# Products of zeros in TensorE's waits ahead of attention's first unit, in place of two memsets, and a fifth block of the second layer ahead of its first output product

## The chip, the cores and the metric

The kernel runs on one core of one Trainium2 chip. The metric is device time of one launch in microseconds (us). The core has TensorE (PE, with PEld for its weight loads), VectorE (DVE), ScalarE (ACT), GpSimd (POOL) and SyncE (SP), which issues most DMAs. Engines run their own instruction lists in order and wait for each other by semaphores.

## The reference, cut to what matters

Three stages follow each other: a gated recurrence (4 batches, 8 heads, 768 steps, 40 dimensions), a mixture of experts in which each of 8 experts takes exactly 384 of 3072 tokens, and a dense two-layer network.

```python
for t in range(S):                                  # attention
    m_new = np.maximum(f_gate[:, :, t] + m, i_gate[:, :, t])
    f_stab = np.exp(f_gate[:, :, t] + m - m_new)
    i_stab = np.exp(i_gate[:, :, t] - m_new)
    C = f_stab * C + i_stab * outer(v_t, k_t);  n = f_stab * n + i_stab * k_t
    y[:, :, t] = sigmoid(o_gate[:, :, t]) * (C @ q_t) / max(abs(n @ q_t), 1.0)
...
for idx in np.argsort(-(x @ w_gate).flatten()):     # routes: best free pair first
    ...
out[mask] = np.maximum(x[mask] @ w1[e], 0.0) @ w2[e]          # per expert e
...
h = x @ w_in                                        # 320 -> 2048
g = np.where(h > 0.0, h, np.exp(np.minimum(h, 0.0)) - 1.0)
return g @ w_out                                    # 2048 -> 320
```

## The kernel before, in words

**Attention** works in 24 units, each 64 steps of 16 of the 32 sequences. For a unit TensorE makes the scores (`scores`, 32 small float32 products into `pS`), the decay matrix (`decay`, into `pF`), the reads of the state (`recall`, into `pR`), the values (`values`, into `pO`) and the new state (`state`, into `pC`). ACT turns the decay matrix into `W` (L321), DVE multiplies scores and `W` into `P` (`weigh`, L360) and copies or adds the new state into `C` (`add_state`, L421 and L419), POOL makes the faded keys `kt`.

Ahead of the units, `__init__` prepares the gates. It starts with `spin(SPIN)`: twelve products of the zero tile `wz` into a scratch bank (L145), which nobody reads. Then the first two time blocks' gates go through DVE (`maximum`, `logs`) and, split into three bfloat16 parts, through ACT and DVE in turns (`split`, L259 to L264, and L267 for `fb`). TensorE's list there is `scores(0)`; `decay(0)` in three pieces, the mask (L315), eight products of `sel` and `fp` (L317) and the one of `fb` (L319); `decay(1)`, which has the same bank `pF` and so waits until ACT has read it (L321); `scores(1)`; then `decays(1, 2)` and the units. DVE's list from there is the gate scan of the remaining steps (L235), the two memsets of the banks `pC` and `pX` (L218, L219), `P` of unit 0, a small product (L328), `P` of unit 1, five wide gate operations (`logs(2, NS)`, L244 to L250), and then the copy of unit 0's state (L421). The first `recall` of TensorE waits for that copy.

**The experts and the dense layers** run in 8 rounds of 384 tokens (TK). `P1` and `C1` are the expert's two layers, `P2` the first dense layer in 16 blocks of 128 columns (eight products of 384 columns each, `up`, L1242), `C2` its second (nine products of 320 columns for a block, L1387, L1388 and L1395). A block of `P2` takes one of four PSUM banks (NPH, `ph`). From the bank, `elu` makes on ACT a relu and an exp into a tile `e` (L1291, L1292; three such tiles), on DVE the sum (L1295, which frees the bank), on ACT or DVE the rounded part `gh` (L1112 or L1114) and on DVE the rest `gl` (L1119, which frees `e`). `C2` takes `gh` for six products, then `gl` for three. There are five tiles each of `gh` and `gl`.

The order is written by a planner. `main` makes a list of blocks: `C2` of block g comes LAG (three) blocks behind `P2`. `Plan` carries a time `t` for TensorE and one for each other engine, from fixed costs per instruction; each `elu` step is put on its engine's list when that time says it is due, and between the products `run` lets other work onto the lists: the routing of later rounds (`routes`, whose products are L805 to L847 and whose DVE steps include `ge`, L630), the splitting of weights and the gathering of rows. In a round the second layer's list begins with `P2` of blocks 0, 1 and 2 interleaved, `P2` 3, `C2` 0, `P2` 4, `P2` 5, `C2` 1, `C2` 2.

Of the kernel before, what the change touches and what calls it, by code (L numbers as in the profile page):

```python
# [31 lines left out]
TG = 20  # L32
NB, NL, PX = 2, 3, 0.2
WARM = [8, 2, 2, 2]


class Plan:
# [50 lines left out]
    def next(self):  # L88
        self.due(min(self.todo)[0])
# [30 lines left out]
class Attention:  # L120
# [4 lines left out]
    def __init__(self, nc, tc, consts, qk, vk, ig, fg, wg, xd, L, ident):  # L125
# [5 lines left out]
        V, G, A = nc.vector, nc.gpsimd, nc.scalar  # L131
# [6 lines left out]
        junk = self.psum("pF", 1)  # L138
        wz = self.wz = one.tile([128, 512], BF, name="wz")
        V.memset(wz, 0.0)  # L140

        def spin(n):

            for _ in range(n):
                nc.tensor.matmul(junk, wz[:, :128], wz, start=True, stop=True)  # L145

        spin(SPIN)
        warm = one.tile([1, 8], F32, name="warm")
        V.memset(warm, 0.0)
# [63 lines left out]
        self.opens(0)  # L213
        self.both(self.scores(0))
        self.load_qk(4)
        self.decay(0)
        self.maximum(128, S)
        V.memset(self.pC, 0.0)  # L218
        V.memset(self.pX, 0.0)  # L219
        self.decay(1)  # L220
        self.both(self.scores(1))
        self.weigh(0)
# [84 lines left out]

        return one

    def decay(self, u):  # L310

        A, PE = self.nc.scalar, self.nc.tensor
        n, bp = divmod(u, 2)
        p = self.psum("pF", 1)
        PE.matmul(p, self.idb, self.low, start=True, stop=False)  # L315
        for h in range(8):
            PE.matmul(p[:, h], self.sel[:, bp * 8 + h].rearrange("p r t -> p (r t)"), self.fp[:, n * 64:n * 64 + 64],  # L317
                      start=False, stop=False)
        PE.matmul(p, self.fb[:, n].rearrange("p r t -> p (r t)"), self.one_m[:, bp * 8:bp * 8 + 8], start=False, stop=True)  # L319
        self.W[u] = self.two.tile([128, 8, 64], F32, name="W", bufs=3)  # L320
        A.activation(self.W[u], p, AF.Exp)  # L321

# [605 lines left out]
class Mlp:  # L928
# [245 lines left out]
    def spin(self, n):  # L1174

        for _ in range(n):
            self.nc.tensor.matmul(self.junk, self.wih[:, 0, :128], self.wih[:, 0, :512], start=True, stop=True)
# [6 lines left out]
    def prep_x(self, r):  # L1184
# [6 lines left out]
        def turn(k):  # L1191
            for t in range(3):
                if (r, t) == (0, 0):
                    self.twice(k, 0)
                nc.tensor.transpose(ps[k][0][:, t * 128:t * 128 + 128], self.xg[k][:, t * 128:t * 128 + 128], self.ident)  # L1195

        def split(k):
            p, slot = ps[k]
            p = p.rearrange("p (t n) -> p t n", t=3)
            h, l = (x[:, :, k * 128:k * 128 + 128] for x in (xh, xl))  # L1200

            def rest():
                nc.vector.tensor_tensor(l, p, h, op=ALU.subtract)
                slot[0] = plan.on("d", 552)
                if k == 2:
                    self.xst[r] = (xh, xl)
                    self.xready[r] = slot[0]

            if r:
                plan.later(self.copy(h, p, 480, 555), rest)  # L1210
            else:
                nc.scalar.activation(h, p, AF.Copy)
                plan.on("a", 480)
                rest()

        if r == 0:
            ps = [self.psum() for t in range(3)]
            for k in range(3):
                self.spin(WARM[k])
                turn(k)  # L1220
                split(k)
            self.spin(WARM[3])
            return
# [208 lines left out]
    def main(self):  # L1432
        plan = self.plan
        LAG = 3
        items = []
        for r in range(NR):
            a, b = [], []
            for f in range(0, 8 + LAG, 2):
                if f < 8:
                    a += [(self.P1, r, f), (self.P1, r, f + 1)]  # L1440
                a += [(self.C1, r, g) for g in (f - LAG, f + 1 - LAG) if 0 <= g < 8]
            for f in range(0, 16 + LAG, 2):
                if f == 0:
                    b.append((self.P2, r, [0, 1, 2]))
                elif f == 2:
                    b.append((self.P2, r, [3]))
                elif f < 16:
                    b += [(self.P2, r, [f]), (self.P2, r, [f + 1])]
                b += [(self.C2, r, g) for g in (f - LAG, f + 1 - LAG) if 0 <= g < 16]
            if r:  # L1450
                tail = items[-LAG:]
                del items[-LAG:]
                items += a[:2] + tail[:2] + a[2:3] + tail[2:] + a[3:]
            else:
                items += a
            items += b
        items[-NL:] = [(lambda r, f: self.C2(r, f, NL), NR - 1, 16 - NL)]
        while items:
            if items[0] == (self.P1, items[0][1], 0) and self.xready.get(items[0][1], 1e18) > plan.t:
                k = next((k for k, x in enumerate(items[:7]) if x[0] == self.C2), 0)  # L1460
                items.insert(0, items.pop(k))
            fn, r, f = items.pop(0)
            if fn in (self.P1, self.C1):
                while r not in self.xst:
                    if self.plan.todo:
                        self.plan.next()
                    plan.t += 50
                    yield "rows" if self.routed >= r else "routes"
                while self.wsplit < 5 * r + (3 if fn == self.P1 else 4 + f // 4):
                    plan.t += 50  # L1470
                    yield "weights"
                if fn == self.P1 and f == 0:
                    plan.wait(self.xready[r])
            if fn == self.C2 and r == 0:
                while self.wdone < f + 1:
                    plan.t += 50
                    yield "wout"
            if fn == self.C1 and f == C0:
                self.rush = True
            g = f[0] if fn == self.P2 else f  # L1480
            self.pos = r + (g / 32 if fn in (self.P1, self.C1) else 3 / 8 + g * 5 / 128)
            yield from fn(r, f)
            if fn == self.C2 and f == C9:
                self.rush, self.prog = False, r
# [227 lines left out]
```

## Time and profile before

| | us |
|---|---|
| median of 3 runs | 749.46 |
| lowest, highest | 748.71, 754.47 |
| profiled execution, its own time | 749.06 |
| its span, first to last instruction | 747.3 |

The span is 1.8 us shorter than that execution's own time; the times below count from the span's start. Attention lasts to about 150 us, the routing of the first round to about 184 us, and the eight rounds fill the rest. TensorE matmul is busy for 697.3 us in 7244 products, with as many weight loads, and the chain of work that ended last is 74% TensorE. In the views, "idle before <- X" is the time an engine had nothing to do before an instruction and what released it; "issue" is a wait for which the profile shows no releaser. The clock column of a stretch is TensorE's granted clock, 1.00 for 2.4 GHz and 0.50 for 1.2 GHz.

### The profile page before, as it was taken

The numbers are of one execution on the slowest core, as the hardware profiler recorded it, in microseconds if no ns is written. First come the engines' busy times: TensorE is split into PE (matmuls) and PEld (weight loads), VectorE is DVE, ScalarE is ACT, GpSimd is POOL, SyncE is SP. The second block draws the span as 40 slices with busy tenths as digits, with TensorE's granted clock in tenths as the row PEclk, the third lists the DMA queues.
The fourth block names the chain that finished last, engine by engine and source line by source line (L and its number), as shares of the span: only waits on it lengthen the run. The fifth ranks groups of instructions, "written<-read, shape, count | busy, mean of one in ns | idle before, by whom it ended". The sixth has DMA issues, their size and how long they took to land.

```text
span 747.3 us, 18041 instructions
## 1 busy us (share of the span) xinstructions
PE 697.3 (93%) x7244; PEld 642.1 (86%) x7244; DVE 552.6 (74%) x1654; ACT 394.3 (53%) x892; POOL 192.2 (26%) x242
## 2 busy tenths in 40 slices
PE   7788889846999999999999999999999999999997
PEld 4566566734989998999899999999999999999997
DVE  7677968876888978996897688768867863752542
ACT  5554544434454726662675367456736763752443
POOL 4655745326211400410121022104100441001001
PEclk9899999956999999999999999999999999999999
DMA  8777967335101400310230023003200531100000
GB/s 277 224 221 223 280 201 232 88 107 184 59 1 41 168 2 1 131 63 17 74 109 28 1 86 97 28 1 111 75 24 0 175 113 68 36 1 27 1 1 26
DMA packets 22435, 67.29 MB, mean 90 GB/s; under 512 B 3536, under 2 KB 7632, under 8 KB 22352
## 3 DMA queue, kind: packets, MB, share of 16 engines
q1 hardware_dynamic: 14240, 35.12, 15.3%
q0 software_dynamic: 8064, 30.94, 12.6%
q8 instruction: 56, 0.92, 0.5%
q14 instruction: 27, 0.22, 0.1%
q10 hardware_dynamic: 48, 0.10, 0.0%
HBM read 58.28 MB, written 7.86 MB: 89 GB/s over the span
## 4 chain that ended last, share of the span: by engine, by line
PE 74%; issue 10%; DVE 9%; ACT 2%; DMA 2%; POOL 1%; POOLq 0%; SPq 0%; DVEq 0%; ACTq 0%
PE ph L1242 30%; PE acc L1395 6%; PE acc L1387 6%; PE acc L1388 6%; PE acc L1343 2%; PE pO L381 2%; PE pR L395 2%; PE acc L1337 2%; PE acc L1338 2%; PE pX L464 2%; PE acc L1335 1%; PE acc L1344 1%; PE pS L306 1%; PE ph L1195 1%; DMA vk<-in_vk_dram 1%
## 5 line engine op out<-in xcount | busy, mean ns | idle before, releaser
L1295 DVE SCALAR_TENSOR_TENSOR e<-e,ph 128x384 f32<-128x384 f32 x128 | 70.2, 549 | 45.9 <-ACT e L1292 45.4
L1291 ACT ACTIVATE e<-ph 128x384 f32<-128x384 f32 x128 | 62.3, 487 | 76.5 <-PE ph L1242 67.3
L1242 PE MATMUL ph<-yh,wih 128*128 128x384 f32 x256 | 87.7, 343 | 0.0
L1242 PE MATMUL ph<-yh,wil 128*128 128x384 f32 x256 | 86.3, 337 | 0.0
L1119 DVE TENSOR_TENSOR gl<-e,gh 128x384 fp32r<-128x384 f32 x128 | 70.0, 551 | 2.3 <-ACT gh L1112 1.0
L1259 ACT ACTIVATE gh<-ph 128x384 fp32r<-128x384 f32 x62 | 30.4, 490 | 74.2 <-PE ph L1242 74.1
L1292 ACT ACTIVATE e<-e 128x384 f32<-128x384 f32 x128 | 67.3, 526 | 4.0
L1424 POOL DMA_INDIRECT out_dram<-ot,idx x24 | 24.7, 1030 | 160.0 <-ACT ot L1112 157.0
L1242 PE MATMUL ph<-yl,wih 128*128 128x384 f32 x256 | 65.2, 341 | 0.0
L1123 POOL DMA_INDIRECT stg<-in_w1a_dram,wi x16 | 15.9, 996 | 191.4 <-DVE wi L864 188.6
L1266 DVE SCALAR_TENSOR_TENSOR gl<-ph,gh 128x384 fp32r<-128x384 f32 x64 | 35.0, 552 | 38.4 <-ACT gh L1259 38.1
L1387 PE MATMUL acc<-woh,gh 128*128 128x320 f32 x186 | 56.2, 313 | 0.0
L1112 ACT ACTIVATE gh<-e 128x384 fp32r<-128x384 f32 x95 | 48.8, 514 | 13.4 <-DVE e L1295 13.2
L1388 PE MATMUL acc<-wol,gh 128*128 128x320 f32 x186 | 55.5, 309 | 0.0
L1387 PE MATMUL acc<-woa,gh 128*128 128x320 f32 x168 | 51.8, 318 | 0.5 <-DVE gh L1114 0.5
L1388 PE MATMUL acc<-wob,gh 128*128 128x320 f32 x168 | 50.4, 309 | 0.0
L1242 PEld LDWEIGHTS ph<-yh,wih 128*128 128x128 f32 x256 | 48.1, 188 | 0.2
L1242 PEld LDWEIGHTS ph<-yh,wil 128*128 128x128 f32 x256 | 48.2, 188 | 0.0
L1242 PEld LDWEIGHTS ph<-yl,wih 128*128 128x128 f32 x256 | 45.4, 188 | 0.0
L1242 PE MATMUL ph<-xh,w1h 128*128 128x384 f32 x128 | 43.6, 341 | 0.7 <-ACT xh L1112 0.7
L1242 PE MATMUL ph<-yh,wis 128*128 128x384 f32 x128 | 44.1, 344 | 0.0
L1242 PE MATMUL ph<-yl,wis 128*128 128x384 f32 x128 | 43.2, 337 | 0.0
(311 smaller groups left out, 2059.4 us busy)
## 6 DMA issues: line engine op xcount, KB each, us to landing
vk<-in_vk_dram SPq DMA_DIRECT2D x24, 484.0 KB, 5.4
qk<-in_qk_dram SPq DMA_DIRECT2D x20, 320.0 KB, 5.0
cx<-in_win_dram SPq DMA_DIRECT2D x8, 512.0 KB, 4.9
xd<-x SPq DMA_DIRECT2D x48, 80.0 KB, 3.6
wx<-in_wout_dram SPq DMA_DIRECT2D x9, 320.0 KB, 2.9
cx<-in_wout_dram SPq DMA_DIRECT2D x5, 448.0 KB, 3.9
qk<-in_qk_dram SPq DMA_DIRECT2D x4, 512.0 KB, 7.1
cx<-in_win_dram SPq DMA_DIRECT2D x4, 256.0 KB, 4.6
```

Of the source, the lines that this page charges most:

```text
L1112: self.nc.scalar.activation(out, x, AF.Copy)
L1119: self.nc.vector.tensor_tensor(out, x, y, op=ALU.subtract)
L1242: PE.matmul(p, w, x, start=k == 0, stop=k == 7)
L1259: nc.scalar.activation(h, p, AF.Relu)
L1266: nc.vector.scalar_tensor_tensor(l, p, 0.0, h, op0=ALU.max, op1=ALU.subtract)
L1291: nc.scalar.activation(e, p, AF.Relu, scale=-1.0)
L1292: nc.scalar.activation(e, e, AF.Exp, scale=-1.0)
L1295: nc.vector.scalar_tensor_tensor(e, e, -1.0, p, op0=ALU.add, op1=ALU.max)
L1387: PE.matmul(p, h[:, c], wh, start=f == 0, stop=False)
L1388: PE.matmul(p, h[:, c], wl, start=False, stop=False)
L1395: PE.matmul(p, l[:, c], wh, start=False, stop=False)
L1424: s = nc.gpsimd.indirect_dma_start(out=self.out, out_offset=bass.IndirectOffsetOnAxis(ap=idx[:, t:t + 1], axis=0), in_=o, in_offset=None)
```

## The change

`spin` gets a bank as its second argument. `decay` gets a callback that is called behind each of its three pieces; for unit 0 it puts four products of zeros there, the first four into `pC`, the next two groups of four into `pX`. Each writes zeros over its whole bank, and the two memsets are taken out. In `main` the block of `P2` number 4 goes in front of `C2` 0 in all eight rounds; the rest of the list keeps its order.

```diff
+WAIT = [4, 4, 4]
...
-        def spin(n):
+        def spin(n, bank=junk):
 
             for _ in range(n):
-                nc.tensor.matmul(junk, wz[:, :128], wz, start=True, stop=True)
+                nc.tensor.matmul(bank, wz[:, :128], wz, start=True, stop=True)
...
-        self.decay(0)
+        self.decay(0, lambda k: spin(WAIT[k], self.pX if k else self.pC))
         self.maximum(128, S)
-        V.memset(self.pC, 0.0)
-        V.memset(self.pX, 0.0)
         self.decay(1)
...
-    def decay(self, u):
+    def decay(self, u, gap=lambda k: None):
...
         PE.matmul(p, self.idb, self.low, start=True, stop=False)
+        gap(0)
         for h in range(8):
...
+        gap(1)
         PE.matmul(p, self.fb[:, n].rearrange("p r t -> p (r t)"), self.one_m[:, bp * 8:bp * 8 + 8], start=False, stop=True)
+        gap(2)
         self.W[u] = self.two.tile([128, 8, 64], F32, name="W", bufs=3)
...
                 elif f == 2:
-                    b.append((self.P2, r, [3]))
+                    b += [(self.P2, r, [3]), (self.P2, r, [4])]
                 elif f < 16:
-                    b += [(self.P2, r, [f]), (self.P2, r, [f + 1])]
+                    b += [(self.P2, r, [g]) for g in (f, f + 1) if g > 4]
                 b += [(self.C2, r, g) for g in (f - LAG, f + 1 - LAG) if 0 <= g < 16]
```

## Rows read from the trace of the kernel before

**Rows 1.** Chain of waits, 0 to 45 us: start us, us, what.
```profile
10.70 1.86 PE pS L306 x32
...
12.65 0.69 DVE P L360
...
17.99 0.41 DVE C L421
...
26.86 2.38 issue
```
**Rows 2.** Timeline of PE, front: start us, us, line, operation, out<-in, count, idle before.
```profile
5.33 1.15 PE L306 MATMUL pS<-qk 64*64 64x64 f32 x32
6.41 0.39 PE L315 MATMUL pF<-low,idb 128*128 128x512 bf16 x1
7.51 0.39 PE L317 MATMUL pF<-fp,sel 96*128 96x64 bf16 x8 [0.71 <-DVE gi L264]
8.63 0.39 PE L319 MATMUL pF<-one_m,fb 96*128 96x512 bf16 x1 [0.72 <-ACT fb L267]
9.88 0.38 PE L315 MATMUL pF<-low,idb 128*128 128x512 bf16 x1 [0.86 <-ACT W L321]
10.09 0.40 PE L317 MATMUL pF<-fp,sel 96*128 96x64 bf16 x8
...
10.63 1.91 PE L306 MATMUL pS<-qk 64*64 64x64 f32 x32
```
**Rows 3.** Stretches: window, length, busy us (instructions) per engine, PEclk, DMA share, GB/s.
```profile
8.00:10.00 2.00, 0.51 (x2) 0.21 (x3) 1.84 (x3) 1.53 (x4) 0.03 (x1) 1.00 1.02 410
11.00:14.00 3.00, 3.00 (x49) 2.42 (x46) 1.35 (x2) 0.59 (x3) 2.64 (x14) 0.50 1.07 412
...
31.00:38.00 7.00, 6.09 (x142) 4.41 (x140) 3.21 (x6) 1.93 (x5) 4.52 (x4) 0.52 0.65 197
```
**Rows 4.** Timeline of DVE, front: the second memset and P of unit 0.
```profile
9.62 0.48 DVE L219 MEMSET pX<- 128x512 f32 x1
10.02 0.66 DVE L360 TENSOR_TENSOR P<-pS,W 128x512 f32<-128x512 f32 x1
```
**Rows 5.** Timeline of PE around C2 of block 0: rounds 0, 1, 2, 3.
```profile
214.12 0.34 PE L1242 MATMUL ph<-yl,wis 128*128 128x384 f32 x1
...
216.90 0.34 PE L1242 MATMUL ph<-yh,wih 128*128 128x384 f32 x1
...
219.45 0.32 PE L810 MATMUL pr<-A,ge 128*128 128x32 bf16 x6
...
287.23 0.34 PE L1242 MATMUL ph<-yl,wis 128*128 128x384 f32 x1
...
289.72 0.34 PE L1242 MATMUL ph<-yh,wih 128*128 128x384 f32 x1
...
358.51 0.34 PE L1242 MATMUL ph<-yl,wis 128*128 128x384 f32 x1
...
360.86 0.34 PE L1242 MATMUL ph<-yh,wih 128*128 128x384 f32 x1
...
428.73 0.34 PE L1242 MATMUL ph<-yl,wis 128*128 128x384 f32 x1
...
430.31 0.34 PE L1242 MATMUL ph<-yh,wih 128*128 128x384 f32 x1
```
**Rows 6.** Waits: engine, line, waited for: us in total, times, longest us.
```profile
PE acc L1395 <- DVE gl L1119: 1.6, 4, 0.7
```
**Rows 7.** Timeline of DVE, round 0: the routing step that L810 reads.
```profile
218.83 0.56 DVE L630 TENSOR_TENSOR ge<-d,kl 128x768 bf16<-128x768 bf16 x1
```
**Rows 8.** Stretches as in rows 3, each ending in a TensorE wait named "issue".
```profile
0.00:27.50 27.50, 21.21 (x478) 14.29 (x478) 22.58 (x49) 14.35 (x30) 16.54 (x47) 0.94 0.80 263
27.50:50.80 23.30, 19.12 (x511) 14.15 (x511) 16.22 (x42) 12.66 (x28) 11.86 (x12) 0.85 0.66 202
```
**Rows 9.** The page's DMA queues: queue, kind: packets, MB, share of 16 engines.
```profile
q8 instruction: 56, 0.92, 0.5%
```

## The prediction

> **What bounds the kernel now.** I read the page first. Nearly three quarters of the chain that ended last is TensorE, so a wait of TensorE that goes is worth its length, and work added to TensorE is free only inside a wait. The change touches two places, and I read each by its own view.
>
> The first is the stretch ahead of attention's first unit. There the chain of waits, read forward, runs through TensorE's scores of unit 1 for 1.86 us, then through DVE, which makes P of unit 1 at 12.65 and works without a break up to the copy of unit 0's state at 17.99 [rows 1]. On TensorE's timeline the same 32 products took 1.15 us for unit 0 at 5.33 and 1.91 for unit 1 at 10.63 [rows 2]. The reader is to see why: between 6.4 and 9.9 TensorE has three pieces of the decay matrix with waits of 0.71, 0.72 and 0.86 us ahead of them [rows 2], it was busy for 0.51 us of the two up to 10.0, and then the granted clock goes from 1.00 to 0.50 and stays there from 11 to 14 [rows 3]. So scores(1) pays for idleness just before it.
>
> The second place is C2 of block 0 in the eight rounds. Block 3's last product and the next block's first stand 2.78 us apart in round 0 (214.12 to 216.90), 2.49 in round 1, 2.35 in round 2 and 1.58 in round 3 [rows 5]; the nine products between them have the same shapes. In rounds 4 to 7 the timeline looks as in round 3. The wait view names gl of DVE as what TensorE's L1395 stood for, 0.7 us at the longest [rows 6]. So the second part can win something in three rounds of eight.
>
> **Part one, the products of zeros: what they cost.** A product of 512 bfloat16 columns holds TensorE for 0.21 us at the full clock (L315 at 9.88, the next piece at 10.09) [rows 2]. Four take 0.84. Behind the mask piece (6.41 + 0.21 = 6.62) they end at 7.46; `sel` began at 7.51. Behind `sel`, eight products of 64 columns, as long as one of 512, from 7.51 to 7.72, they end at 8.56; `fb` began at 8.63. Behind `fb` (8.84) they end at 9.68; decay(1) began at 9.88, released by ACT [rows 2]. All twelve lie in waits, with 0.05, 0.07 and 0.20 us to spare. Cost: nothing. Without that cover, at half clock, each would take twice 0.21, and four 1.68: 0.79, 0.77 and 0.64 us too late, 2.2 us in all. That is the bound above.
>
> **What they bring.** They add 12 x 0.21 = 2.5 us of work to the stretch that preceded the fall of the clock. If it stays at 1.00, scores(1) takes 1.15 instead of 1.91: 0.76 us, on the chain. What comes next on DVE depends on P of unit 1 and runs back to back to the state's copy [rows 1], so `recall` can start that much sooner. I take 0.75; the bound below the cost is nothing, where the clock falls all the same. The next scores and the zero products after 12.5 also get shorter, but DVE is what ends last there: nothing more.
>
> **The memsets.** The second runs at 9.62, 0.48 us, and P of unit 0 follows it at 10.02 [rows 4]; both memsets gone bring P forward by at most 0.15 us, to the end of W. Nobody gains: DVE's next step on the chain waits for scores(1) until 12.65 [rows 1]. If that cover were gone too, it would be a gain of up to 0.4. I take nothing. The load of unit 4's values hangs on P of unit 1 and is issued 0.75 us sooner, but DMA is full there (share 1.07) [rows 3], so it lands no sooner; POOL's and the other queues keep their order.
>
> **Part two, block 4 ahead of C2 0.** No product is added. TensorE gets eight products of block 4 (about 1.4 us: 8 x 0.17) to do while gh and gl of block 0 are made, and the longest wait above the undisturbed 1.58 is 1.20. Block 4 needs block 0's bank, which DVE frees before it makes gh of block 0, and C2 0 waited for gh anyway; so block 4 starts no later than C2 0 did. Five tiles of gh and gl hold blocks 0 to 4, just enough. Behind it stand P2 5 and C2 1 as before. At most it wins 1.20 + 0.91 + 0.77 = 2.9 us.
>
> What is late next? In round 0 the routing's product L810 follows at 219.45 [rows 5], and its operand ge ends on DVE at 218.83 + 0.56 = 219.39 [rows 7]: TensorE already stood for DVE there. DVE's list up to ge does not hang on C2, so if L810 keeps its place, it takes round 0's gain back; round 1 has such a product right behind its block 5. Round 2 has none. So the lower end is 0.77 if the place is kept, 0 if the planner's new order puts another wait there, and 2.9 if L810 moves back. Rounds 3 to 7: nothing. I take 1.8, midway between 0.77 and 2.9.
>
> **Sum.** 0.75 + 1.8 = 2.55 us off the profiled execution's 749.06 gives 746.5. That execution is 0.4 below the median of the runs shown; on the median's scale 746.9.
>
> **What else moves: TensorE's waits named "issue".** Twelve products bring 24 instructions, a weight load and a matmul each. One of the chain's longest pieces is an "issue" of 2.38 us in the middle of unit 2's products, at 26.86 [rows 1]. The counts show where such waits sit: up to it TensorE has 478 + 478 records, up to the one that ends the second stretch another 511 + 511, close to four times 256 (a few records can be missing) [rows 8]; the page's instruction queue moves 0.92 MB in 56 packets [rows 9], some 259 of the page's 2 x 7244 TensorE instructions to one. So TensorE waits for its code, at block ends. The 24 instructions move every later block end back by 24 instructions' worth of program. After the wait at 26.86 the clock fell too: 0.52 from 31 to 38 [rows 3]. Price of one such wait: 2.4 us alone, and with 7 us at half clock, of which 6.1 busy and slowed by 1.91/1.15 = 1.66, another 6.1 x (1 - 1/1.66) = 2.4: between 2.4 and 4.8, and I take 3.7.
>
> The Trainium skill says, under "Runtime: NRT & Kernel Launch", Instruction fetch mechanics, that code comes in 16 KiB blocks of 256 instructions while the last is executed, and that crossing a block's end is mostly hidden. By that rule the 24 instructions would cost nothing, and the sum stays 746.9. The trace agrees on the size and not on the hiding (2.38 us).
>
> **Rivals.**
> 1. Both parts are taken back. The next code block's arrival sets attention's pace, so that the 0.75 us only lengthen the wait at 26.86, and L810 takes part two's gain. For: the wait exists and two of three rounds have an L810 close behind. Against: round 2 has none. Between 748.7 and 749.5.
> 2. Slower: the moved block ends put one more long code wait on the chain, in attention, where code and loads share the DMA engines. For: nothing ties the ends to a good place. Against: the number of ends does not change. 746.9 + 3.7 = 750.6, at most 751.7. It decides the sign from one net wait; two would make 754 to 757.
> 3. The same move takes the wait at 26.86 away: its code would be asked for ahead of unit 2's loads. 746.9 - 3.7 = 743.2, at most 742.1.
> 4. In some executions the clock is still at half when the new products run, so they overrun by up to 2.2 us and the front gains nothing: 746.9 + 0.75 + 2.2 = 749.9. For: only the twelve first products ahead of scores(0) have brought it up. Against: scores(0) took 1.15 us at 5.33, the short time, and the clock stood at 1.00 from 8 to 10 [rows 2, 3].
>
> **How the numbers follow.** Forecast 0.50, rivals 0.18, 0.15, 0.14 and 0.03. The likeliest alone spans 745.8 (2.9 and 0.75 won) to 748.7. The range takes in rivals 2 and 3 with their far prices: 742.1 to 751.7, rounded to 742 and 752; what lies outside is two net code waits either way. About 1%, 7.5 us, is what a measurement can tell from no change. Faster than 742.0 needs everything and more than one code wait removed: 0.05. Slower than 757.0 needs two added and the gains lost: 0.03. Else 0.92.
>
> **What would show each step.** Right: no fall of the granted clock between 10 and 14 us, scores(1) near 1.15 us, the state's copy near 17.2; no wait ahead of L1395 of block 0 in rounds 0 to 2. Wrong: `sel` or `fb` later than 7.5 and 8.6 (products overrun); an "issue" longer than 2.4 ahead of 30 us (rival 1 or 2) or none (rival 3); L810 of round 0 still at its old distance from the round's start (part two taken back).

## The result, and the profile after

| kernel | median of the runs shown | ratio to before, 95% interval | profiled execution | its span |
|---|---|---|---|---|
| before | 752.23 us | | 749.06 us | 747.3 us |
| after | 761.12 us (757.54 to 763.97) | 1.0123 [1.0087, 1.0158] | 757.54 us | 755.8 us |

The kernel became slower by 1.2%, where 746.9 us had been forecast. The 8.48 us between the two profiled executions can be laid out by marks that are easy to find on TensorE's timeline. They are the first product of `P1` in round 0, the first product of `P2` in each round, and the last product of `C2`. From the start to the first `P1` (all of attention and the first routing) after takes 184.72 us, before 184.68; that they are so close is chance, as the scatter in the table of the experiments shows. To the first `P2` it loses 0.33 us, and behind the last `C2` 0.20 us. Everything else, 7.91 us, lies between the first `P2` and the last `C2`, where before takes 534.28 us. The same table cuts that stretch by rounds. The loss is in three of them: 2.44 us in round 0, 3.30 in round 2 and 4.17 in round 4. Rounds 1 and 3 became shorter by 1.06 and 0.91 us.

The waits of TensorE from 205 to 735 us show what stands there now. Columns: engine, tile, line and what it waited for, then us in total, times, longest.

```profile
PE acc L1417 <- DVE gl L1121: 4.0, 2, 2.0
PE acc L1337 <- DVE w L1121: 2.1, 1, 2.1
...
PE acc L1413 <- ACT gh L1114: 0.8, 2, 0.4
PE pr L849 <- DVE flag L662: 0.8, 1, 0.8
```

The row of [rows 6], `C2` waiting for gl of DVE (four times, 0.7 at the longest), is gone: block 4 did fill those waits. In their place stand three long ones, twice 2.0 us for the low half of block 15 at the end of a round, and once 2.1 us for a weight split. A routing product waits in round 0 too, L849 for `flag`, 0.8 us. It is not the one that was expected there: L812, the L810 of before, does not stand in the list.

The end of round 2 on TensorE's timeline (start us, us, line, operation, tiles, count, idle before):

```profile
399.74 0.41 PE L1413 MATMUL acc<-woh,gh 128*128 128x320 f32 x1 [0.42 <-ACT gh L1114]
399.99 0.30 PE L1414 MATMUL acc<-wol,gh 128*128 128x320 f32 x1
402.31 0.63 PE L1417 MATMUL acc<-woh,gl 128*128 128x320 f32 x1 [2.01 <-DVE gl L1121]
```

and what DVE did meanwhile:

```profile
400.11 0.15 DVE L836 TENSOR_REDUCE fs<-flag 32x1 f32<-32x8 bf16 x1
400.18 1.61 DVE L1121 TENSOR_TENSOR w<-stg,w 128x256 fp32r<-128x256 f32 x3
401.72 0.54 DVE L1121 TENSOR_TENSOR gl<-e,gh 128x384 fp32r<-128x384 f32 x1
```

Three splits of the next round's weights, 1.61 us, stand on DVE's list ahead of the one low half, 0.54 us, that the last `C2` of this round needs. The order was written by the planner when it built the kernel, and DVE keeps to it. In before, DVE has one split of 0.42 us and two low halves of the next round's `P1` there, and block 15's low half comes at 399.75:

```profile
398.26 0.42 DVE L1119 TENSOR_TENSOR w<-stg,w 128x256 fp32r<-128x256 f32 x1
398.59 1.24 DVE L1266 SCALAR_TENSOR_TENSOR gl<-ph,gh 128x384 fp32r<-128x384 f32 x2
399.75 0.55 DVE L1119 TENSOR_TENSOR gl<-e,gh 128x384 fp32r<-128x384 f32 x1
```

TensorE reads it only at 403.13, because its own list differs there as well:

```profile
401.45 0.34 PE L1242 MATMUL ph<-xh,w1h 128*128 128x384 f32 x1
...
402.84 0.31 PE L1411 MATMUL acc<-woh,gh 128*128 128x320 f32 x1
```

Three blocks of the next round's `P1` (from 395.78 on, the third at 401.45) stand ahead of block 15's `C2` in before. In after the first `P1` of the next round comes behind all of `C2`, at 404.34: `main` pulls `C2` ahead where, by the planner's times, the next rows are not ready yet. So moving one block rewrote TensorE's own list as well. In round 4 before has all of `C2` ahead of `P1` too, and no such wait: its low half of block 15 stands at 538.09, ahead of the splits at 538.56 and 540.20. The wait in after has a second price. The stretches (window, length, busy us and count of PE, PEld, DVE, ACT, POOL, granted clock, DMA share, GB/s):

```profile
399.70:402.00 2.30, 0.56 (x2) 0.30 (x2) 2.20 (x8) 0.30 (x1) 0.00 (x0) 1.00 0.00 0
402.00:405.40 3.40, 3.09 (x11) 3.09 (x12) 2.11 (x7) 1.48 (x5) 1.49 (x3) 0.50 0.07 23
405.40:410.00 4.60, 4.60 (x33) 4.43 (x32) 2.83 (x12) 1.59 (x5) 1.66 (x3) 1.00 0.26 95
```

TensorE was idle for most of 2.3 us, and then the clock was granted at 0.50, the lower of its two levels (1.2 GHz), for 3.4 us. Its products of 384 columns start 0.32 us apart there, and 0.17 in the rest of the round. In before the same time runs at 1.00:

```profile
400.00:403.40 3.40, 3.40 (x28) 3.30 (x27) 1.24 (x7) 0.36 (x1) 0.00 (x0) 1.00 0.00 0
```

So the place costs 0.42 + 2.01 us of waiting and, by estimate from these distances, some 11 x 0.15 = 1.6 us of slow products. Round 2 lost 3.30 us in all, since it had won some 0.6 at its first `C2`, as the runs below show. The end of round 4 repeats it at 542 us. The third place, the weight split in round 0, begins on POOL. First its timeline in after, then in before:

```profile
250.00 1.02 POOL L1125 DMA_INDIRECT xg<-xd,idx  x1 [0.30 <-PE pr L746]
251.02 0.09 POOL L1425 MEMSET spc<- 1x1 f32 x1
256.18 1.01 POOL L1426 DMA_INDIRECT out_dram<-ot,idx  x1 [5.07 <-ACT ot L1114]
257.49 1.44 POOL L1125 DMA_INDIRECT stg<-in_w2a_dram,wi  x1 [0.30 <-issue]
```
```profile
250.44 1.32 POOL L1123 DMA_INDIRECT stg<-in_w2a_dram,wi  x1 [0.31 <-issue]
253.21 1.01 POOL L1123 DMA_INDIRECT stg<-in_w2a_dram,wi  x1 [1.46 <-DVE w1l L1119]
...
256.65 1.31 POOL L1424 DMA_INDIRECT out_dram<-ot,idx  x1 [2.34 <-ACT ot L1112]
```

In after the gather of the next round's weights stands behind the first store of this round's rows. The store waits 5.07 us for its rows, so the gather goes out at 257.49 instead of 250.44. The chain of waits of after runs through both:

```profile
251.11 4.84 issue
257.49 4.66 DMA stg<-in_w2a_dram,wi
```

**The front.** Here nothing came of the forecast 0.75 us. TensorE and DVE in after:

```profile
1.21 5.13 PE L146 MATMUL pF<-wz 128*128 128x512 bf16 x12 [1.21 <-DVE warm L150]
6.27 1.15 PE L305 MATMUL pS<-qk 64*64 64x64 f32 x32
7.58 1.03 PE L146 MATMUL pC<-wz 128*128 128x512 bf16 x4
...
9.76 1.03 PE L146 MATMUL pX<-wz 128*128 128x512 bf16 x4
...
11.38 1.15 PE L305 MATMUL pS<-qk 64*64 64x64 f32 x32
```
```profile
12.65 0.69 DVE L362 TENSOR_TENSOR P<-pS,W 128x512 f32<-128x512 f32 x1 [1.13 <-PE pS L305]
17.91 0.48 DVE L423 COPY C<-pC 128x328 f32<-128x328 f32 x1
```

Scores(1) did take 1.15 us, but began at 11.38 instead of 10.63 [rows 2], so P of unit 1 is made at 12.65, the very time of before [rows 1].

### The profile page after: what moved, and what is told of

Its sections match the earlier page's. It is cut to its first block, busy times and chain, and to the rows that moved or that the text cites. A ratio compares the mean times of both kernels' runs of the same rounds, so it can differ in the third digit from the quotient of the medians.

```text
span 755.8 us, 18078 instructions
## 1 busy us (share of the span) xinstructions
PE 698.9 (92%) x7252; PEld 644.3 (85%) x7256; DVE 557.3 (74%) x1663; ACT 389.3 (52%) x881; POOL 186.6 (25%) x242
## 4 chain that ended last, share of the span: by engine, by line
PE 69%; DVE 13%; issue 11%; ACT 3%; POOL 2%; DMA 1%; POOLq 0%; DVEq 0%; ACTq 0%
PE ph L1244 27%; PE acc L1389 5%; PE acc L1397 5%; PE acc L1390 5%; PE acc L1345 2%; PE acc L1339 2%; PE acc L1340 2%; PE pO L383 2%; PE pR L397 2%; PE pX L466 2%; PE acc L1337 1%; DMA stg<-in_w2a_dram,wi 1%; PE acc L1346 1%; DVE w L1121 1%; PE pS L305 1%
## 5 line engine op out<-in xcount | busy, mean ns | idle before, releaser
L1114 ACT ACTIVATE gh<-e 128x384 fp32r<-128x384 f32 x90 | 46.0, 515 | 12.5 <-DVE e L1297 12.4
L1244 PE MATMUL ph<-xh,w1l 128*128 128x384 f32 x128 | 43.5, 340 | 0.0
```

The costliest lines, as they stand in the source:

```text
L1114: self.nc.scalar.activation(out, x, AF.Copy)
L1244: PE.matmul(p, w, x, start=k == 0, stop=k == 7)
```

## Experiments

Three theories were put against each other first. Theory 1: the planner places all other work by the list that was edited, so it wrote new lists for DVE, ACT and POOL, and these carry the loss. (SP's list is the same in both kernels.) Theory 2: the 24 instructions move the ends of the code blocks. Theory 3: TensorE's new order itself, first of all block 4 ahead of `C2` 0. (Later expectations call theory 1 theory L.) This table gives, for every kernel that was profiled, the first product of `P1` (us from the start), then the time from the first `P2` of each round to that of the next (the last column of these to the last `C2`), and their sum, all read from TensorE's timeline of one execution each.

| kernel | first P1 | 0 | 1 | 2 | 3 | 4 | 5 | 6 | 7 | sum | ratio to before, 95% interval |
|---|---|---|---|---|---|---|---|---|---|---|---|
| before | 184.68 | 73.32 | 71.13 | 70.88 | 70.08 | 70.16 | 68.47 | 66.85 | 43.39 | 534.28 | |
| after | 184.72 | 75.76 | 70.07 | 74.18 | 69.17 | 74.33 | 68.54 | 66.78 | 43.36 | 542.19 | 1.0123 [1.0087, 1.0158] |
| fill_only | 190.74 | 73.24 | 71.13 | 70.84 | 70.17 | 70.16 | 68.47 | 66.85 | 43.40 | 534.26 | 1.0019 [0.999, 1.0048] |
| fill_again | 191.00 | 73.27 | 71.13 | 70.89 | 70.07 | 70.17 | 68.46 | 66.83 | 43.43 | 534.24 | 1.0028 [0.9998, 1.0058] |
| shift_only | 190.37 | 73.29 | 71.12 | 70.85 | 70.14 | 70.16 | 68.46 | 66.83 | 43.40 | 534.26 | 1.003 [1.0001, 1.006] |
| block_only | 186.07 | 77.57 | 70.06 | 74.37 | 69.14 | 74.50 | 68.44 | 66.71 | 43.29 | 544.10 | 1.0124 [1.008, 1.0169] |
| swap_only | 185.99 | 73.31 | 71.11 | 70.27 | 69.99 | 70.05 | 68.43 | 66.79 | 43.36 | 533.33 | 0.9978 [0.9953, 1.0004] |
| swap_again | 185.01 | 73.27 | 71.10 | 70.25 | 70.07 | 70.08 | 68.44 | 66.80 | 43.38 | 533.38 | 0.9977 [0.9949, 1.0004] |
| fill_swap | 186.01 | 73.36 | 71.15 | 70.28 | 70.00 | 69.99 | 68.40 | 66.79 | 43.36 | 533.33 | 1.0002 [0.9974, 1.003] |
| store_last | 185.22 | 73.57 | 70.07 | 74.33 | 69.24 | 74.40 | 68.51 | 66.78 | 43.36 | 540.26 | 1.0107 [1.0071, 1.0143] |
| split_last | 189.78 | 77.50 | 70.08 | 72.10 | 69.24 | 72.09 | 68.48 | 66.78 | 43.30 | 539.58 | 1.0129 [1.0086, 1.0172] |
| lists_mended | 187.62 | 73.45 | 70.07 | 72.07 | 69.22 | 72.08 | 68.46 | 66.71 | 43.37 | 535.44 | 1.0063 [1.0033, 1.0093] |
| split_spread | 184.08 | 73.45 | 70.08 | 71.33 | 69.14 | 71.32 | 68.52 | 66.78 | 43.36 | 533.98 | 1.0017 [0.9987, 1.0047] |
| late_only | 183.59 | 73.30 | 71.13 | 70.83 | 69.13 | 74.39 | 68.46 | 66.71 | 43.30 | 537.25 | 1.0043 [1.0, 1.0087] |
| r1_only | 185.38 | 73.31 | 70.08 | 72.31 | 70.06 | 70.47 | 68.46 | 66.84 | 43.39 | 534.92 | 1.0004 [0.998, 1.0029] |
| r3_only | 186.50 | 73.30 | 71.11 | 70.85 | 69.23 | 72.32 | 68.49 | 66.82 | 43.40 | 535.52 | 1.0015 [0.9992, 1.0039] |
| r1_swap | 184.30 | 73.28 | 70.08 | 72.31 | 70.18 | 70.47 | 68.46 | 66.84 | 43.40 | 535.02 | 1.002 [0.9998, 1.0041] |

The table itself is the main find. Up to the first `P1` the kernels lie between 183.6 and 191.0 us. From the first `P2` on, kernels with the same lists agree to some 0.05 us in the sum (before, the two fill kernels and shift_only: 534.24 to 534.28) and 0.2 us in a round. So a loss or gain of half a microsecond in the rounds can be read from one execution, while one in attention is lost in scatter and needs the ratios. There is one exception, round 0 with the long wait for the weight split: after takes 75.76 us, block_only and split_last, whose lists in that round are the same, 77.57 and 77.50. In these two the granted clock fell to 0.50 behind the wait of 2.24 and 2.19 us, in after it stayed at 1.00 behind one of 2.13 us.

### The two parts alone: fill_only, block_only

Each takes one of the diff's two halves: fill_only all but the last hunk, block_only that hunk alone.

> The change's first part alone: the twelve products of zeros in place of the two memsets; the order of the second layer's blocks as before. Theory 1 (the loss of the whole change sits in the second part, in the instruction lists that the planner writes for DVE and ACT): within 2 us of the kernel before, ratio 0.997 to 1.003, and no new wait of TensorE behind 184 us. Theory 2 (the 24 added TensorE instructions move the code block ends in attention): 3 to 9 us slower, all of it ahead of 150 us. Theory 3 (TensorE's own new order is worse): as theory 1 here.

> The change's second part alone: block 4 ahead of the first output product in the planner's list, memsets kept, no products of zeros. Theory 1: 6 to 10 us slower than before (ratio 1.008 to 1.013), with waits of 2 us and more for DVE at the round ends near 264, 400 and 543 us as in the whole change. Theory 2: 1 to 3 us faster. Theory 3: as theory 1 here.

block_only loses what after loses (1.0124 against 1.0123), and its waits are those of after, shifted by a few us. In the rounds it is 9.82 us against 7.91, and 1.8 us of the difference are round 0's stretch at half clock. fill_only keeps before's rounds to 0.1 us. The loss is that of the moved block.

### TensorE's order without the planner's: swap_only, swap_again, fill_swap

The planner is left with before's list, and TensorE's products of `C2` 0 are only handed out behind block 4 (`Held` keeps the calls, `flush` makes them). DVE, ACT, POOL and SP have before's lists, instruction for instruction (in fill_swap those of fill_only).

```diff
             wh, wl = self.wo(f)
+            if f == 0:
+                PE = self.hold = Held(PE)
...
                 self.elu(r, fs[k], *p)
+                if fs == [4]:
+                    self.hold.flush()
```

> Kernel before, with the planner run exactly as before, so that DVE, ACT, GpSimd and SyncE have the same lists instruction for instruction; only TensorE's list differs: the nine products of the first output block stand behind block 4 instead of ahead of it, in all eight rounds. Theory 1: 1 to 3 us faster than before (0.996 to 0.999), the waits ahead of the gl products of block 0 gone in rounds 0 to 2. Theory 3: 6 to 10 us slower, as the whole change. Theory 2: 1 to 3 us faster.

> The products of zeros together with the swap on TensorE's list alone (the other engines' lists as with the first part alone). Theory 1: 1 to 4 us faster than before, the best of the four. Theory 2: 1 to 8 us slower. Theory 3: 6 to 10 us slower.

> TensorE's new order with before's lists on every other engine once more, now with more rounds: 0.9978 [0.9953, 1.0004] before. By the forecast's part two with the gains of rounds 0 and 1 partly taken back by the routing products, 0.6 to 1.8 us less: ratio 0.9976 to 0.9992.

The three sums are 533.33 to 533.38, 0.9 us under before's. Theory 3 falls for the order that was edited: block 4 ahead of `C2` 0 is a small gain. (The two ratios, 0.9978 and 0.9977, do not quite exclude 1, and fill_swap, at 1.0002, did not come out faster as theory 1 had it; the gain is read from the rounds.) Theory 2 falls as the cause of the loss, since fill_swap has the 24 instructions and the gain in the rounds. Theory 1 stands: with before's lists on the other engines nothing of the 8 to 10 us is left. These kernels do not have what the planner changed on TensorE's own list at the ends of rounds; split_spread, below, has that.

The gain is also where the prediction had put it. Rounds 0 and 1 keep before's times, round 2 is 0.6 us shorter. TensorE's waits of swap_only, 208 to 600 us, name what took the first two back:

```profile
PE pr L824 <- DVE ge L644: 1.3, 2, 1.0
PE pr L861 <- DVE flag L674: 1.0, 1, 1.0
```

Both are routing products, L824 being the L810 of before and L861 its L847. In round 1 L824 stands 1.03 us for ge, right behind block 5. In round 0 it is not L810 that waits, as had been forecast, but L861, for `flag`: in before the six gh products of `C2` 0 stood ahead of that product, and without them TensorE comes to it 0.96 us too early. The routing kept its times: counted from the first `P2` of round 0, the `flag` product starts at 7.46 us in before and 7.40 in swap_only, the one that reads ge at 11.44 and 11.43.

### One list at a time: store_last, split_last, lists_mended, late_only

These start from after and move single instructions on other engines, TensorE's order being that of after. In store_last the stores of round 0 go behind the two gathers:

```diff
+                if r == 0 and self.stores is not None:
+                    self.stores.append(store)
+                else:
+                    store()
...
                     self.get_w(r, 4)
+                    for store in self.stores or []:
+                        store()
+                    self.stores = None
```

> The kernel after, with one thing moved on GpSimd's queue alone: in round 0 the three stores of the round's rows stand behind the two gathers of w2 for round 1 instead of around them. Theory L (the planner's new lists on the other engines carry the loss, each at one place): in the trace of after the first gather is issued at 257.49 behind a store that waited 5.07 us for its rows, against 250.44 in before, and C1 of round 1 waits 2.13 us for the split of what it fetched. With the stores behind, the gathers go out at about 251 and 254, the wait at 264 goes, the second layer of round 1 begins at 281.3 to 282.2 instead of 284.15, and the time falls by 2 to 3 us: ratio to before 1.008 to 1.010. Rival (the wait for the split comes from the split lists of VectorE and ScalarE, whatever the gather does): the wait at 264 stays within 0.5 us and the ratio stays at 1.012.

```profile
251.78 1.43 POOL L1125 DMA_INDIRECT stg<-in_w2a_dram,wi  x1 [0.30 <-DVE neg L752]
254.65 1.02 POOL L1125 DMA_INDIRECT stg<-in_w2a_dram,wi  x1 [1.44 <-DVE w1l L1121]
```

The gathers go out at 251.78 and 254.65, the wait of 2.13 us ahead of 266.58 is gone, and round 0 takes 73.57 us instead of 75.76, against 73.32 in before. That is the whole loss of that place but 0.25. (The ratio fell by 0.0016 only, and its interval holds after's 1.0123. Of the 2.2 us, 0.9 is lost again in this execution behind the last `C2`, 6.08 us against 5.19.)

In split_last the splits that fall between the ELU of block 15 and its low half are held back and issued behind the low half, in rounds 2 and 4:

```diff
         mine = self.es.take(False)
+        if f == 15 and r in (2, 4):
+            self.held = []
...
             mine[0] = self.minus(l, e, h, 590)
+            if f == 15:
+                self.flush()
```

> The kernel after, with one thing moved on VectorE's and ScalarE's queues alone: in rounds 2 and 4, weight splits that the planner put between block 15's ELU and its low half are issued behind that low half. Theory L: TensorE's waits at the ends of these rounds (399.7 to 402.3 and 542.4 to 545.7, 2.5 to 3 us each) and the stretches at half clock behind them (3.4 us each, worth 1.7) go; the second layer of round 3 begins 3 us earlier against round 2 than in after, that of round 5 4 us earlier against round 4, and the time falls by 6 to 8 us: ratio 1.002 to 1.005. Rival (the splits are what the next round's first layer needs next, so a split moved back makes that layer wait as long): the idle time moves from block 15 to the first layer's products of rounds 3 and 5 by 2 us or more each, and the ratio stays at 1.009 to 1.013.

The waits of 2.0 us for gl went, and with them the two stretches at half clock, but rounds 2 and 4 became shorter by only 2.1 and 2.2 us of the 3.3 and 4.2 lost. The waits from 205 to 735 us show a new one:

```profile
PE pr L812 <- DVE ge L632: 3.3, 2, 1.6
PE acc L1348 <- DVE w L1128: 2.2, 1, 2.2
```

The splits that were put back now stand ahead of ge, for which a routing product waits, once in each of the two rounds. This is neither theory as it was written: the wait did not move to the first layer, but to routing. (The ratio of 1.0129, from four runs, did not fall and misses theory L's 1.002 to 1.005. In the profiled execution 5.06 us more than in after were gone by the first `P1`, and round 0 had the stretch at half clock, 1.7 us.)

> The kernel after with both: the stores of round 0 behind the gathers, and the splits of rounds 2 and 4 behind block 15's low half. TensorE's order is that of after. Theory L: the whole loss is in these three places, so the kernel comes to 749 to 752, ratio 0.998 to 1.002, and the second layer of round 7 begins within 1.5 us of before's 698.9. Rival (part of the loss lies elsewhere in the changed lists): the ratio stays above 1.004 with the three waits gone.

With both, the sum is 535.44, 6.75 of the 7.91 us recovered. What is left in the rounds are the two waits for ge, 1.64 us in round 2 and 1.65 in round 4:

```profile
399.32 0.54 DVE L1128 TENSOR_TENSOR gl<-e,gh 128x384 fp32r<-128x384 f32 x1
399.78 3.15 DVE L1128 TENSOR_TENSOR w<-stg,w 128x512 fp32r<-128x512 f32 x6
...
404.00 0.56 DVE L632 TENSOR_TENSOR ge<-d,kl 128x768 bf16<-128x768 bf16 x1
```

The ratio of 1.0063 is above the range that theory L had set (0.998 to 1.002), and above the 1.004 of its rival: the three waits were not the whole. Of the 3.96 us by which this execution's end stands behind before's, 2.94 are there before the first `P1`, in attention.

> The kernel before, with block 4 ahead of C2's first only in rounds 3 to 7, where before shows no wait ahead of that C2 to be filled. Theory L: nothing is gained, and the planner's lists lose what they lose: by the built order, VectorE's list at the end of round 2 is before's and at the end of round 4 is after's (three splits ahead of block 15's low half). So rounds 0 to 2 run as before, 4 us are lost between the second layers of rounds 4 and 5, and the ratio is 1.004 to 1.007. Rival (the loss is that of moving the block, some 1.2 us a round wherever it is moved): five of eight rounds, spread evenly, ratio 1.007 to 1.008. Second rival (the loss follows rounds 0 to 2, where the wait was filled): ratio 1.000.

late_only loses 4.23 us in round 4, as theory L had it, gains 0.95 in round 3, and neither in rounds 5 to 7, where the block is moved as well. An even loss per moved block is out, and so is a loss tied to the filled wait: round 4 has no wait at `C2` 0 to fill.

### The six splits spread: split_spread

As lists_mended, but only the first part of the six splits goes behind gl, the rest ahead of the next round's first `C1`.

```diff
             if f == 15:
-                self.flush()
+                self.flush(NOW)
```

> As lists_mended, but of the six splits that stood together behind block 15's low half in rounds 2 and 4 the last ones are issued only ahead of the first C1 of the next round. In lists_mended the six take VectorE from 399.78 to 402.86 and the comparison of routing (ge, L632) comes at 404.00, for which a routing product held up TensorE for 1.64 us in each of the two rounds. Theory L: with the splits behind it ge comes about 1 us earlier, these waits fall to 0.2 to 0.9 us each, and the stretch from the second layer of round 0 to the end falls from 540.4 to 538.5 to 539.5 us (before 539.3, after 547.4). Rival (the wait is for the routing chain itself): the 1.64 us stay.

The waits for ge fell to 0.7 us each:

```profile
PE pr L813 <- DVE ge L633: 1.4, 2, 0.7
```

From the first `P2` to the end it takes 538.97 us, within what theory L expected, and the sum is 533.98, 0.3 under before's. TensorE's order is still that of after, its rewritten ends of rounds included, so this order is not enough to lose anything. The loss in the rounds needs the planner's new lists on the other engines, and it can be undone by moving a few stores and splits on POOL, DVE and ACT. (The ratio, 1.0017, cannot be told from 1.)

### Why one round loses and the next gains: r1_only, r3_only, r1_swap

The block goes ahead in one round alone, through the planner.

```diff
+EARLY4 = (1,)
...
-                    b.append((self.P2, r, [3]))
+                    b += [(self.P2, r, [3])] + [(self.P2, r, [4])] * (r in EARLY4)
```

> The kernel before, with block 4 ahead of C2's first in round 1 alone, by the planner. In all kernels with the planner's new lists the stretch from the second layer of round 1 to that of round 2 takes 70.07 us against 71.13 of before. If that 1.06 us belongs to round 1's own list, it stays here (70.1) and the rest is before's: from the second layer of round 0 to the last C2 533.2 us against 534.3. If the list of a round depends on the state that the round before left, round 2 changes too (by the built order its list at the end is neither before's nor after's): 2 to 4 us more there when splits come ahead of block 15's low half, none when not; the built order has none directly ahead of it, so I expect 533.2 to 534.

> The same in round 3 alone, where before shows no wait ahead of C2's first to be filled. If the 0.9 us by which after and all replanned kernels are shorter from round 3 to round 4 (69.2 against 70.1) is a matter of the list alone, it comes here too: 69.2 there, and 533.4 us from the second layer of round 0 to the last C2; if it needs the earlier rounds' changes, 70.1. Round 4's list is then the one that round 2 has in r1_only, so both cost or neither.

> r1_only with TensorE's order alone changed in rounds 0 and 2 as in swap_only (every other engine's list is that of r1_only): 0.6 us less in round 2, round 0's gain taken back: 532.5 us from the second layer of round 0 to the last C2, against 534.3 of before. Over the whole kernel 0.9975 of before, if attention's part scatters evenly.

Round 1 alone gains its 1.05 us, and then round 2, where nothing was edited, loses 1.43. Round 3 alone gains 0.85, and round 4 loses 2.16. The sums, 534.92 and 535.52, miss what was expected (533.2 to 534, and 533.4). A round's list is thus a matter of the state in which the round before left the planner. In both kernels one wait is new, in r1_only at 387.52 and in r3_only at 529.39 us, for the split of the next round's rows:

```profile
PE ph L1245 <- DVE xl L1206: 1.0, 1, 1.0
```

It is the larger part of the 1.43 us and about half of the 2.16; where the rest is lost is not shown. r1_swap shows the same from the other side: with round 2's list changed, TensorE's new order brings nothing there (72.31 in both). Its ratio, 1.002, is not the 0.9975 that was expected. In no run was the gain of round 1 or 3 kept without a loss in the round behind it; split_spread comes nearest.

### Part one: shift_only

Before, with 24 instructions more on TensorE and no filler:

```diff
         spin(SPIN)
+        for _ in range(12):
+            nc.tensor.matmul(junk[:, 0, :16], wz[:, :128], wz[:, :16], start=True, stop=True)
```

> The kernel before with twelve small products of zeros (16 columns each) behind the spin at the very start, where TensorE idles until 7.5 us anyway: as many instructions more as the fillers bring, and nothing else of the change. Theory C (the fillers' small loss of some 2 us is that of code: 24 instructions more on TensorE put the ends of its code blocks at other products): the trace has a wait of 2 to 5 us of the kind the page calls issue ahead of a decay product at 53 to 58 us, as each of the six traces with fillers has and none of the four without, and the ratio is that of fill_again, about 1.002. Theory F (the fillers cost where they stand, by holding up decay and scores): no cost here, ratio 1.000, fill_again 1.002. Third possibility (the loss of part one is scatter between executions): both ratios within 0.002 of 1.000.

> Part one alone once more (the fillers and the two memsets away), for its size beside shift_only on the same chip: 1.0019 [0.999, 1.0048] before; by theories C and F 1.001 to 1.003, by the forecast 0.999 (-0.75 us).

The two ratios are the same, 1.003 and 1.0028; only the interval of shift_only excludes 1, and by a hair. Twelve products that fill nothing cost what the fillers cost. The waits called "issue" from 50 to 60 us, shift_only, fill_again and before:

```profile
PE pF L319 <- issue: 1.8, 1, 1.8
```
```profile
PE pF L317 <- issue: 3.5, 1, 3.5
```
```profile
PE pS L306 <- issue: 2.2, 1, 2.2
PE pR L395 <- issue: 0.9, 1, 0.9
```

The nine traces with the 24 instructions all have such a wait ahead of a decay product there, of 1.8 to 4.8 us, and none of the eight without has; these wait ahead of a score product, as before does. It is the same place in the code. Counted over weight loads and matmuls, the waits named "issue" longer than 0.5 us between 12 and 185 us, 127 in the seventeen traces, all stand 194 or 195 records behind a multiple of 256 (190 to 193 in after, whose trace lacks a few records). Each ends 1.2 to 1.7 us after one of the 16384-byte packets of the instruction queue [rows 9] has landed. So these waits are for code, at block ends, as the prediction had read them, and 24 more instructions put each block end ahead of another product. Added up from 12 to 185 us, the waits called "issue" are 10.2 us on average without the 24 instructions (7.4 to 13.6) and 12.3 with them (10.3 to 15.0). The first `P1` stands at 185.2 on average without (183.6 to 186.5) and at 187.7 with (184.1 to 191.0). The difference fits, 2.2 and 2.5 us, but the ranges overlap, and the profiled execution of after is one of the short ones (184.72). That part one costs about 0.2%, and that the moved block ends are the reason, is thus likely and not proven. What the two runs of part one alone leave little room for is a gain: 0.75 us would be a ratio of 0.999, the lower end of fill_only's interval and outside that of fill_again.

## Why the prediction was wrong, point by point

**The step that failed.** Part two's account ends with "Behind it stand P2 5 and C2 1 as before", and its bounds with "0 if the planner's new order puts another wait there". The account followed TensorE's list at `C2` 0 and took the rest, the other engines' lists above all, for fixed; the possibility that they are not was named, priced at nothing gained, and given no loss. The planner places every split, store and gather by the times of the list that was edited. The runs showed three waits in its place, 2.01 us twice for a low half behind three splits and 2.13 us for a weight split whose gather stood behind a store, and two stretches at half clock: 7.9 us lost in after's rounds and 9.8 in block_only's, in a term for which a gain of 0 to 2.9 us had been forecast. None of the rivals is this one. Rival 2 forecast a loss, but by code and in attention, of 3.7 us; its case of two such waits ended at 757, under the 761.12 that came.

**The rest of part two was right in kind.** With the lists held, the waits of [rows 5] were filled, routing products took rounds 0 and 1 back (in round 0 the one that waits for `flag`, not L810), and round 2 kept 0.6 us, for which 0.77 had been written. The term measured 0.9 us. The 1.8 of the sum was the middle between 0.77 and 2.9, and the step "if L810 keeps its place" should have decided it: its place is kept, at 11.43 us from the round's start against 11.44, which the prediction itself had named as the sign of a gain taken back.

**Fillers cost nothing: wrong.** The margins of 0.05, 0.07 and 0.20 us were those of one execution, in which the twelve first products took 4.08 us and scores(0) stood at 5.33 [rows 2]. In after they took 5.13, and over all seventeen traces 4.08 to 5.30. Where scores(0) comes at 6.0 to 6.4 us, as it does in seven of the eight traces that have neither the fillers nor shift_only's products (before is the eighth), there is less to fill: the wait ahead of `sel` is at most 0.06 us instead of 0.71, and the three together come to 1.1 to 2.1 us, under the 2.5 of the fillers. Those then hold up decay and scores one behind the other. In seven of the eight traces with fillers the copy of the state begins 11.64 to 11.65 us behind scores(0), in the seven just named 10.7 to 11.5. The copy stood at 17.8 us on average in the eight with fillers (17.05 to 18.38) and at 17.4 in the other eight (16.98 to 17.92); that is 0.4 us between two ranges that overlap.

**They bring 0.75 us: wrong, but for one case.** Scores(1) at 1.91 us was taken for the rule. swap_again, without a filler, has

```profile
6.44 1.30 PE L320 MATMUL pS<-qk 64*64 64x64 f32 x32
...
10.95 1.15 PE L320 MATMUL pS<-qk 64*64 64x64 f32 x32
```

and so have seven of the eight; of these only the profiled execution of before, with its early scores(0), met the half clock of [rows 3]. (shift_only, with scores(0) at 5.59, met it too: 1.75 us.) In most executions there was hardly anything to win. In the one trace with fillers in which scores(0) comes about as early as in before, it went as the account had it: fill_swap has it at 5.41, decay(1) begins at 9.77 (9.88 in before), the clock stays at 1.00 from 11 to 14 us, scores(1) takes 1.15 us, and the copy begins at 17.05, 0.87 us ahead of before's 17.92. The other signs that were named came as well: in all eight traces with fillers the clock stays up from 11 to 14 us and scores(1) takes 1.15 us. They came without a gain: scores(1) began at 11.3 us on average with the fillers, and at 10.8 in the seven.

**The memsets** were not tried alone. In fill_swap unit 0's `P` stands at 9.73 us instead of 10.02, and unit 1's `P` still waits 1.13 us for scores(1), so nothing came of it there, as forecast.

**"What else moves" was right in kind.** The prediction read the waits called "issue" as code, and their places in all traces bear that out; rival 2 let the 24 instructions put one more long wait into attention, at 3.7 us. shift_only shows a cost of 0.3% [0.01, 0.6], some 2 us. The Trainium skill, "Runtime: NRT & Kernel Launch", Instruction fetch mechanics, has the crossing of a code block mostly hidden; by it shift_only would cost next to nothing, and its wait of 1.8 us and, by a hair, its ratio speak against that here. Rival 3 did not come: in after 0.90 us are left of the wait of 2.38 at 26.86 [rows 1], at the same block end, but other waits grew, and the first `P1` stands where it stood. One pair of executions cannot show more: among the traces without the 24 instructions that wait is anything from under 0.5 to 2.38 us. Of rival 1, routing took back the gain of rounds 0 and 1. Rival 4 had the clock late, but its fillers at half clock; in after it is the twelve products ahead of them that ran slowly, while the fillers ran four in 1.03 us.

**The sum.** 749.06 - 2.55 was forecast for the profiled execution, and 757.54 came: 11.0 us apart. Of these, 7.91 + 0.9 is the planner's lists (the gain of TensorE's order alone taken as 0.9 and lost in them too), another 0.9 the gain of part two that was set too high, 0.75 that of part one, and 0.57 lies ahead of the first `P2` and behind the last `C2`. On the medians, 746.9 and 761.12, it is 14.2 us: the profiled execution was the fastest of its six, 3.6 us under their median, and that scatter lies in attention as far as the other traces show.

## What to carry to other kernels

Where a planner writes the queues, no edit of one engine's list is local: compare the built lists of all engines before and after, the edited one too, and look on each queue for what has come to stand ahead of the instruction that the bound engine waits for next. To learn what an order is worth by itself, hold back its instructions at the end and leave the planner as it was. And before a wait is filled, look at whether it is the same in a second execution.

## What the runs showed of the hardware

The start differs from execution to execution more than expected: the same twelve products, begun at 1.21 us in all traces, took from 4.08 to 5.30 us. Without fillers the clock fell at 11 us in two of nine traces, those with the shortest two times, 4.08 and 4.17 us; whether that is the reason was not tested. The first `P1` stands between 183.6 and 186.5 us in the eight traces without the 24 instructions and between 184.1 and 191.0 in the nine with them, while the eight rounds behind repeat to within 0.1 us where the lists are the same and the clock does not fall.

TensorE waited for its code at block ends of 256 instructions, 127 times for more than 0.5 us between 12 and 185 us of the seventeen traces, and went on 1.2 to 1.7 us after the block had landed.

An idle time of some 2 us in the rounds can cost nearly double. After the waits of 2.01 us at the ends of rounds 2 and 4 the granted clock was 0.50 for 3.4 us, in after twice and in block_only and store_last likewise. The wait for the weight split in round 0 was followed by it in block_only (0.65 on average from 268.5 to 272.0) and split_last, but not in after, so the length of the wait alone does not decide it.

A store on POOL that waits for its rows holds up the gathers behind it on that list: 5.07 us in after, for which TensorE stood 2.13 us later; with the stores behind the gathers that wait was gone.
